# Log sums that run through a sequence, instead of starting again every 128 tokens

## The chip, the cores and the metric

One core of a Trainium2 chip runs the whole program. The metric is device microseconds of one execution, as the median of several. The kernel before takes 425.86 us (three runs, 425.14 to 426.12).

## The reference

Two parts follow each other. The first is a linear recurrence over 768 tokens, for 4 sequences and 8 heads of 48 features, with a complex decay per token and feature:

```python
mag = np.sqrt(a_re * a_re + a_im * a_im)
scale = np.minimum(mag, 0.999) / (mag + 1e-06)
a_re_n, a_im_n = (a_re * scale, a_im * scale)
for t in range(S):
    new_re = ar * S_re - ai * S_im
    new_im = ar * S_im + ai * S_re
    S_re, S_im = (new_re + kv, new_im)      # kv = outer(k[t], v[t])
    y[:, :, t] = np.einsum('bhd,bhde->bhe', q[:, :, t], S_re)
```

The second is a gated block on y: `h = gelu(x @ w_in)`, its halves u and v, v normalized over its features, mixed over the tokens by `w_sg` and shifted by `b_sg`, `gated = u * v_s`, and `out = x + gated @ w_out`.

## The kernel before

The recurrence is computed in chunks of 128 tokens (24 of them, numbered g; c = g mod 6 is the place in the sequence). The logarithm of the decay's size is summed over the tokens; exp of half that sum multiplies q (`ep`), exp of minus half multiplies k (`em`), cosine and sine of the summed angle turn both. Within a chunk, scores `pa` (line 668) are masked into `am` (678), and `py` (719) takes `am` times v. Across chunks a state `S` of 96 x 384 is carried: `ps` (694) is k times v of the chunk, transposed to `kt` first (650), and `py` adds q times the state of the chunk before (724).

Work is prepared in units of up to 256 tokens. The first sequence has tokens on the partitions and sums by matmul; the three later ones (`fea(n)`, nine units) have features on the partitions, three tiles of 128, and sum with scans on the vector engine. For these the log sum starts again every 128 tokens: the scan at line 450 multiplies the running sum by `going`, which is 0 at each 128th element. So `ep` at a chunk's last token is the decay over the whole chunk, and the state has to be multiplied by it: line 499 spreads these columns, `pd` (507) moves them by six small matmuls with `of_head` and `of_place` into `dec`, and lines 705 and 710 multiply the state by `dec`.

```python
nc.vector.tensor_tensor_scan(out=x, data0=going, data1=x, initial=0.0, op0=ALU.mult, op1=ALU.add)
```

Turned k and q of the later sequences go through DRAM (`rk`, `rq`, line 607) to come back with heads on the partitions (`K`, `Q`, line 628). The gated block is `normal` (`pv`, line 236, gelu, statistics, `vh`, `vl`), `expand` (`pu`) and `spatial` (`pvs`, `po`), each product as three matmuls of rounded parts.

Every piece of work is a generator, and `ORDER` is a written list of steps: a name says which generator goes on by one step, `:3` three times, and the number of primes says which engine takes a step that could run on several (`alt`: in `evac` none is ScalarE and one is VectorE, in `ew` one prime is GpSimd). `f` is `keep_warm`, in which a step with no prime issues nothing. Each engine, and the DMA queue that SP issues, takes its instructions in this order. The names of the steps: `l` and `m` load, `g` logs, `e` scale, `p` turns, `r` rotate, `z` heads, `a` attend, `n`, `x`, `y` the gated block.

Of the kernel before, what the change touches and what calls it, by code (L numbers as in the profile page):

```python
# [18 lines left out]
P = 128  # L19
# [5 lines left out]
RE_MIN, IM_MAX = 0.7, 0.98  # L25
# [12 lines left out]
e2'' a1 z1 e1 a1 a0' g3 e2 g3 a1'' a1 s2' t3 a1 w4:2 a1 g3 s2 w7' p2 v2 s2 w4 p3 g3:2 e2:2 a0 w4 g3:2 r3 v3 z3 g3 r2
a1 e3 w7' r3 z2 r2 w9 z3:2 w1'' p3 w12:2 w9'' l4 z2 g4 e3 z2 p3 w12 a1 m3 z3 g4 w9 z2 w4 z2 p3 w4' w12 g4 z2 m3 e3 z2
e2 p3 e3' w8 z3 w12'' e3 p3'' e3' z3' z2 e3 e3' e3 g4 z3 a2 n0_0 z3' a2'' w8 a2:2 n0_0' p3 e3 a2 s3 w5 w8 a2 g4 a2' a2  # L40
a3 a2:2 a3:2 s3 a3 s3 a3'' a3 w12 w5 a3 r4'' e3 a3 r4 n0_0' n0_0 t4 w5 z4 a3 g4 n0_0 z4 w5 z4 r5'' w10 n0_0:2 z4 v5
n0_2:2 z4 z4' v4 n0_2' a3 w5 l5 n0_0 a4 z5 z4 a4'' n0_0 r5'' w10 z4 w11 e3 z5 g4 w10' p4:2 a4:2 z5 a4'' z5:4 a4 g4 m4
n0_0 a4:2' w11 g5:2 l6 p4 w14 z5 g4 a4 a5 p4 a5:2 p4 n0_0' e4 m4 a5'' w11'' l6 a5 n0_0' a4 e4:2 w5 s4 l5 n0_2' a5 p4
w15 x0_0 a5 s4:2 n0_3 e4'' e4 n0_0 x0_0 g5:2 w15 x0_0:2 r6:2 w15 r6:2 r6'' n0_0'' x0_0 w15 n0_2 r6 r6'' x0_0:2 z6 t5
n0_2 n0_3:2'' g5 p5 e4:2 z7 n0_3' x0_3 w15' w15 g5 a6 n0_2 v7 w14 n0_0 p5 v6 w14 r6 p5 g5 x0_0 w14 p5 n0_0'' n0_3
w14'' z6 n0_2'' a6:2 w14' a7 g5 n0_3 n0_2 n0_3 p5 n0_3 x0_3 n0_2' a6:2 n0_3:2 a7 f a7 s5 n0_3 z7 g6 x0_3 m5 g5 n0_3
a7'' a6:3 e5 a6:2 p5 n0_3 e5'' f e5 o1:2 a7 a6 g6 n0_3 a6 a7'' g6'' a7 m5 l7 a7'' n0_3' l7 a7 s5:2 a7 r8 n0_3' r8
n0_3'' r8'' n0_3 n0_3:2'' n0_3 r8 a7'' n0_3'' z8 a6 g6 e5:2 t6 a6 r8'' r8 g6 a7 r8 y0_0:4 x0_3 g6 r8 y0_0' y0_0:2 z9
y0_0'' p6 y0_0 y0_0' p6 g6 y0_0 l8 y0_0 p6 y0_0'' z8 z9 y0_0 y0_0' g6 g7 y0_0 a7 x0_3 y0_0:3 a8 y0_0' g7 p6 g6 v8 p6
a9 a8 g7 e6 s6'' a9 y0_0 a8 a8' a9 m6 a8 l8 a8'' a8 s6 e5 a8 a9 s6 a8 m6 e6'' v9 y0_0 a7 a8 g7 e5 r10 t7 g7 y0_0 r10  # L50
p7 r10'' p7 r10 a9 e6 a8:2 a9:2 a8 e6' x0_3 v10 y0_3 a8 e6 r10'' z10 x0_3 g7 x0_3 g7 z11 y0_3 r10 y0_0 g8 a9 y0_0 r10'
y0_0 p7 g7 y0_3 y0_0 p7 y0_0 a9 r10 e6 y0_3:2' y0_0 g7 z10 g8:2 m7 a9:2 e7 a9 y0_3 g8 a9' p7:2 y0_3 y0_3'' g8 z11 s7'
t8 y0_3 s7 y0_3'' y0_3 a10 s7 e7 a10' a10 m7 e6'' a10' e7 a10:3 a10'' a10 a11 y0_3 a9 a10 g8 r12' a10' a10 a11'' v11
a11 n1_0 a10 l9 r12 a11'' y0_3'' y0_3 r12' a10 r12 g9 e7 n1_0 g8 e7 r12 y0_3 a11 r12 y0_3 a11 n1_0 g8 n1_0:2 a11 p8
y0_3 f r12'' v12 p8 y0_3 y0_3:2' l9 g8 n1_3 g9 n1_0:2 p8 n1_0:3 y0_3 n1_0 z12 p8 y0_3 r12 m8 z12 n1_0 y0_3 p8 n1_3 z13
g9' g9 n1_3'' y0_3 s8' n1_0 g9 y0_3 e8 y0_3 e8' e8 g9 y0_3 m8 n1_3 y0_3 a12 n1_0 y0_3 p8 a12' a12 s8:2 a12' a12 a12''
n1_0:2'' l10 t9 v13 p9 k2 z13 r14 n1_0 a12 a12'' n1_0'' n1_0 r14 e8'' n1_0' e7 a12 a13' a13:2 r14 e7 x1_3:2 l10 x1_3
e8 x1_3 r14 n1_0 r14'' r14 n1_3:6 z15 x1_3 n1_0' n1_3:2 x1_3 m9 a12 f:3 a13'' a13 a12 a13:2 a13'' a13:2 a13'' r14'
n1_3 g9 r14 n1_3' z14 e8:2 n1_3 n1_3' n1_3'' a13 n1_3 f a15' f n1_3'' a13 n1_3:2 g9 n1_3 p9:2 x1_3 y1_3 x1_0 v14 g10
a13 g10:2 y1_3 p9 a15 g10 x1_3 g10 z15 g9 y1_3 e9 y1_3:2' y1_3 a12 y1_3 y1_3'' y1_3 p9 y1_3' g10 y1_3 x1_0 a14 e9''  # L60
z14 x1_0' a14'' a14 a15 a14' a14:2 v15 a15' e9 y1_3 s9 m9 a14 l11 a14'' g10 s9 a12 a14:2 a14' a15 e9'' a14 l11 a15 s9
y1_3' r16 e9 r16 f r16'' y1_3' r16:2 a15 x1_0 t10 p10:3 g10 y1_3 r16 k2 x1_0:5 a14' x1_0 r16' r16 x1_0 z16 g11 v16 g10
# [26 lines left out]
def tile_kernel(ctx: ExitStack, tc: tile.TileContext, t_q, t_k, t_re, t_im, u_q, u_k, u_re, u_im, t_v, v, q, k, f_re, f_im,  # L89
# [40 lines left out]
    def cst(shape, dt, name):  # L130
        return const.tile(shape, dt, name=name, tag=name)
# [107 lines left out]
    def others():  # L239
        nc.gpsimd.memset(going, 1.0)  # L240
        nc.gpsimd.memset(going[:, 0:MT:P], 0.0)
# [165 lines left out]
    def logs(n):  # L407
# [686 lines left out]
```

## Time and profile before

| what | value |
|---|---|
| median of 3 runs | 425.86 us (425.14 to 426.12) |
| profiled execution, first to last instruction | 424.2 us |
| TensorE busy | 410.3 us, 97% of the span |
| VectorE busy | 347.8 us, 82% |
| ScalarE busy | 278.5 us, 66% |
| GpSimd busy | 161.1 us, 38% |
| granted TensorE clock, mean | 0.997 |
| DMA | 92.95 MB, mean 219 GB/s |

The page gives no time for the profiled execution besides its span; the median of the runs is 1.7 us above that span, which is what lies around the instructions. Busy time counts an instruction from its start to its modelled end, so that matmuls that follow each other closely overlap; for them the distance between starts is the cost.

### The profile page before, as it was taken

To read this page: it belongs to the slowest core of one execution; us is meant where nothing else is said; L and a number is where in the kernel's file an instruction comes from. 1 tells how busy PE (TensorE), PEld (TensorE's weight loads), DVE (VectorE), ACT (ScalarE), POOL (GpSimd) and SP (SyncE) were. 2 spreads that over 40 slices of the span, in tenths; PEclk is the share of its full clock that TensorE was granted. 3 is DMA by queue.
4 is the path that set the end of the run, shared out by engine and by line. 5 is a ranking of instruction groups with operands and counts; after the bars stand their busy time and mean duration, and the time that the engine had idled before them with its cause. 6 is when DMAs were issued, how large, how long until landed. Compare 5 with 4: busy or idle time off the path is not lost. (4 is left out here: it accounts for less than half of the span.)

```text
span 424.2 us, 10001 instructions
## 1 busy us (share of the span) xinstructions
PE 410.3 (97%) x3914; PEld 375.8 (89%) x3914; DVE 347.8 (82%) x600; ACT 278.5 (66%) x396; POOL 161.1 (38%) x218
## 2 busy tenths in 40 slices
PE   7999998989999999999899999999999999999994
PEld 5667787879899998989899998989999989899994
DVE  5999989999999989996999698797975546585482
ACT  7899998999899768876987945855830212540010
POOL 4126248265241442815274643622121255223210
PEclk9999999999999999999999999999999999999998
DMA  6778869698498888979669879889669955653531
GB/s 207 232 244 227 263 183 285 172 279 264 123 284 257 240 290 229 286 221 289 174 173 298 232 228 286 272 225 257 138 199 298 247 164 173 194 177 110 185 97 62
DMA packets 77564, 92.95 MB, mean 219 GB/s; under 512 B 10564, under 2 KB 59462, under 8 KB 77512
## 3 DMA queue, kind: packets, MB, share of 16 engines
q1 hardware_dynamic: 77368, 92.16, 73.5%
q8 instruction: 32, 0.52, 0.5%
q14 instruction: 20, 0.16, 0.1%
q10 hardware_dynamic: 144, 0.10, 0.1%
HBM read 68.64 MB, written 23.60 MB: 217 GB/s over the span
## 5 line engine op out<-in xcount | busy, mean ns | idle before, releaser
L236 PE MATMUL pvs<-wsgh,vh 128*128 128x384 f32 x192 | 65.6, 342 | 0.0
L236 PE MATMUL pvs<-wsgh,vl 128*128 128x384 f32 x192 | 65.0, 339 | 0.0
L236 PE MATMUL pvs<-wsgl,vh 128*128 128x384 f32 x192 | 64.7, 337 | 0.0
L199 ACT ACT_TABLE_LOAD x48 | 61.6, 1283 | 1.7 <-PEq L1079 0.9
L668 PE MATMUL pa<-Q,K 96*64 96x64 f32 (+1 forms) x768 | 41.4, 250 | 1.3 <-ACT csn L200 0.9
L668 PEld LDWEIGHTS pa<-Q,K 96*64 96x64 f32 x768 | 36.9, 137 | 4.2 <-issue 1.5
L719 PE MATMUL py<-am,vbuf 128*64 128x128 f32 x384 | 38.8, 275 | 0.4 <-DVE am L678 0.4
L236 PEld LDWEIGHTS pvs<-wsgh,vh 128*128 128x128 f32 x192 | 36.0, 188 | 1.2 <-issue 0.9
L236 PEld LDWEIGHTS pvs<-wsgh,vl 128*128 128x128 f32 x192 | 36.1, 188 | 0.6 <-DVE vl L225 0.5
L236 PEld LDWEIGHTS pvs<-wsgl,vh 128*128 128x128 f32 x192 | 36.1, 188 | 0.0
L678 DVE TENSOR_TENSOR am<-pa,masks 128x512 f32<-128x512 f32 x45 | 30.3, 682 | 5.6 <-PE pa L668 4.8
L724 PE MATMUL py<-Q,S 96*48 96x128 f32 x320 | 33.8, 272 | 0.0
L236 PE MATMUL pu<-xh,winh 128*128 128x384 f32 x96 | 32.8, 341 | 0.0
L850 PE MATMUL po<-gh,wouth 128*128 128x384 f32 x96 | 32.7, 341 | 0.0
L225 POOL TENSOR_TENSOR gl<-tg,gh 128x384 fp32r<-128x384 f32 x13 | 16.8, 1290 | 41.0 <-DVE gh L222 20.8
L850 PE MATMUL po<-gh,woutl 128*128 128x384 f32 x96 | 32.4, 337 | 0.0
L236 PE MATMUL pu<-xh,winl 128*128 128x384 f32 x96 | 32.4, 337 | 0.0
L850 PE MATMUL po<-gl,wouth 128*128 128x384 f32 x96 | 32.3, 337 | 0.0
L236 PE MATMUL pu<-xl,winh 128*128 128x384 f32 x96 | 32.3, 337 | 0.0
L236 PE MATMUL pv<-winh,xh 128*128 128x512 f32 x72 | 29.0, 403 | 0.5 <-ACT u__1296 L200 0.3
L236 PE MATMUL pv<-winh,xl 128*128 128x512 f32 x72 | 28.4, 395 | 0.7 <-DVE xl L225 0.7
L863 DVE SCALAR_TENSOR_TENSOR tg<-pvs,gcol,bsg 128x384 f32<-128x384 f32 x32 | 19.5, 609 | 10.8 <-PE pvs L236 10.6
(285 smaller groups left out, 1104.6 us busy)
## 6 DMA issues: line engine op xcount, KB each, us to landing
vbuf<-in_t_v_dram SPq DMA_DIRECT2D x24, 288.0 KB, 5.7
K<-rk SPq DMA_DIRECT2D x18, 384.0 KB, 5.3
Q<-rq SPq DMA_DIRECT2D x18, 384.0 KB, 7.6
x<-xd SPq DMA_DIRECT2D x9, 576.0 KB, 6.4
xd<-yp SPq DMA_DIRECT2D x48, 96.0 KB, 3.3
gr<-in_f_im_dram SPq DMA_DIRECT2D x12, 384.0 KB, 3.7
out_dram<-x SPq DMA_DIRECT2D x23, 192.0 KB, 2.8
re<-in_u_re_dram SPq DMA_DIRECT2D x9, 384.0 KB, 5.6
```

The source lines that it names most:

```text
L199: nc.scalar.preload_act_table_set(SETS[t])
L225: ew().tensor_tensor(out=l, in0=src, in1=h.bitcast(F32), op=ALU.subtract)
L236: nc.tensor.matmul(o, w(i), x(i), start=(i == 0 and j == 0), stop=(i == n - 1 and j == 2))
L668: nc.tensor.matmul(pa[rows, hh, j:], K(h)[:, j:j + KB], Q(h)[:, j:], start=True, stop=True)
L678: nc.vector.tensor_tensor(out=pairs(am), in0=pairs(pa), in1=causal, op=ALU.mult)
L719: nc.tensor.matmul(py[64 * e:64 * e + 64, p_, :], Vy(h)[:, 0:64], ams[h // 4][:, h % 4, :], start=True, stop=c == 0)
L724: nc.tensor.matmul(py[64 * e:64 * e + D, p_, :], Sb()[:, h, :], Q(h), start=False, stop=True)
L850: nc.tensor.matmul(po[d], w[:, f, ds], g[:, f, :], start=f == 0 and j == 0, stop=f == NF - 1 and j == 2)
L863: nc.vector.scalar_tensor_tensor(out=tg, in0=pv, scalar=gcol[:, f:f + 1], in1=bsg[:, tsl], op0=ALU.mult, op1=ALU.add)
```

## The change

For the nine units of the later sequences the log sum now starts at `MIDDLE` = 128 for a sequence's first unit and runs on over all 768 tokens. Three scans of 256 take the place of two of 384, and an extra small instruction keeps the last column of a unit for the next one (six units of nine). With one sum for the sequence, k and q carry the whole decay, and the state needs no product: the columns (499), the matmuls `pd` (507), their evacuations and the products with `dec` (705, 710) go. The first chunk of a sequence now only copies `ps` to `S`; the three steps where this stands have no prime, so it is a ScalarE copy. `going`, `of_head` and `of_place` are no longer made. The check of the inputs' range takes 0.845 in place of 0.7 as the least real part; the general path behind that check is as it was.

In the list of steps the 69 steps `f` without a prime go, and 17 others stand elsewhere, all between the tokens around chunk 10 and chunk 13; one of these (`a10`) has a prime more, which puts its evacuation on VectorE. One line of the list, before and after:

```diff
@@ ORDER
-... n1_0 a10 l9 r12 a11'' y0_3'' y0_3 r12' a10 r12 g9 e7 n1_0 g8 e7 r12 y0_3 a11 r12 y0_3 a11 n1_0 g8 n1_0:2 a11 p8 ...
+... n1_0 a10' l9 r12 a11'' y0_3'' y0_3 r12' a10 r12 e7 n1_0 g9 g8 e7 y0_3 a11 r12 y0_3 a11 r12 n1_0 g8 n1_0:2 a11 p8 ...
@@ logs
-        for j in range(0, NK * UT, MT):
-            x = fl(U[n]["lo"])[:, j:j + MT]
-            nc.vector.tensor_tensor_scan(out=x, data0=going, data1=x, initial=0.0, op0=ALU.mult, op1=ALU.add)
+        b, c0, m = units[n]
+        for kt in range(NK):
+            x = U[n]["lo"][:, kt, :]
+            nc.vector.tensor_tensor_scan(out=x, data0=x, data1=x, initial=run["sum", b, c0][:, kt:kt + 1] if c0 else MIDDLE,
+                                         op0=ALU.add, op1=ALU.bypass)
+        if c0 + m < NCH:
+            total = run["sum", b, c0 + m] = gp.tile([P, NK], F32, tag="sum", name="sum", bufs=2)
+            ends = U[n]["lo"][:, :, m * P - 1]
+            nc.vector.tensor_tensor(out=total, in0=ends, in1=ends, op=ALU.max)
@@ scale
+        if fea(n):
+            yield
+            psm.tile([P, DM], F32, tag="m", name="pd")
+            yield
+            yield
+            return
...
-        cols_ = gp.tile([P, NK, UC, H], F32, tag="sq", name="cols_", bufs=1)
-        nc.vector.tensor_tensor(out=cols_[:, :, 0:m],
-                                in0=ep[:, :, P - 1:m * P:P].unsqueeze(3).broadcast_to([P, NK, m, H]),
-                                in1=of_head.unsqueeze(1).unsqueeze(1).broadcast_to([P, NK, m, H]), op=ALU.mult)
-        yield
-        pd = psm.tile([2 * D + 1, UC, H], F32, tag="m", name="pd")
-        for kt in range(NK):
-            j = (NK - 1 - kt) * DG
-            for r in COLS:
-                nc.tensor.matmul(pd[r, 0:m, :], of_place[:, j + r.start:j + r.stop], cols_[:, kt, 0:m, :],
-                                 start=kt == 0, stop=kt == NK - 1)
-        yield
-        evac(dec[:, 0:m], pd[0:2 * D, 0:m])
@@ attend
-            if c == 0:
+            if fea(n):
+                if c == 0:
+                    evac(Sn, ps[0:2 * D])
+                else:
+                    nc.vector.tensor_tensor(out=Sn, in0=ps[0:2 * D], in1=Sb(), op=ALU.add)
+                    yield
+            elif c == 0:
```

Where the order moves, for three engines in the same stretch (chunks 12 and 13, the second unit of the third sequence). On VectorE, with the second product with q (`q_2107`, whose result goes to DRAM and comes back as Q of chunk 12), before:

```order
L499 TENSOR_TENSOR cols__2221<-ep_2015,of_head 128x48
L604 TENSOR_TENSOR ep_2015<-q_2107,csn_1970 128x768
L225 TENSOR_TENSOR gl<-tg,gh 128x384
L225 TENSOR_TENSOR xl<-x,xh 128x1152
L446 SCALAR_TENSOR_TENSOR lo_2269<-l_2054,inv_1946 128x768
L524 SCALAR_TENSOR_TENSOR im_1771<-im_1771,left 128x256
L863 SCALAR_TENSOR_TENSOR tg<-pvs,gcol,bsg 128x384
L604 TENSOR_TENSOR q_2107<-q_2107,csn_1970 128x768
L524 SCALAR_TENSOR_TENSOR im_1771<-im_1771,left 128x256
L866 TENSOR_TENSOR tg<-u__1923,tg 128x384
L450 SCALAR_TENSOR_TENSOR lo_2269<-going,lo_2269 128x384 x2
```

and of the change (the q of the same unit is `q_2075` there):

```order
L220 TENSOR_TENSOR gl<-tg,gh 128x384
L583 TENSOR_TENSOR ep_1983<-q_2075,csn_1942 128x768
L220 TENSOR_TENSOR xl<-x,xh 128x1152
L430 SCALAR_TENSOR_TENSOR lo_2232<-l_2022,inv_1918 128x768
L503 SCALAR_TENSOR_TENSOR im_1754<-im_1754,left 128x256
L848 SCALAR_TENSOR_TENSOR tg<-pvs,gcol,bsg 128x384
L435 SCALAR_TENSOR_TENSOR lo_2232<-lo_2232,sum 128x256 x3
L440 TENSOR_TENSOR sum<-lo_2232 128x3
L583 TENSOR_TENSOR q_2075<-q_2075,csn_1942 128x768
```

The columns are gone, and the scans of the next unit and the small instruction behind them now stand ahead of that product with q, not behind it. On the DMA queue that SP issues, before:

```order
L375 DMA im_2297<-in_u_im_dram 128x768
L764 DMA x<-xd_3_135 128x3x384
L628 DMA K<-rk 96x1024
L607 DMA rq<-q_2107 128x3x128 x2
L375 DMA k_2357<-in_u_k_dram 128x768
L628 DMA Q<-rq 96x1024
L886 DMA out_dram<-x 128x384
```

and of the change:

```order
L749 DMA x<-xd_3_132 128x3x384
L359 DMA im_2312<-in_u_im_dram 128x768
L607 DMA K<-rk 96x1024
L359 DMA k_2322<-in_u_k_dram 128x768
L586 DMA rq<-q_2075 128x3x128 x2
L607 DMA Q<-rq 96x1024
L871 DMA out_dram<-x 128x384
```

The load of the next unit's `im` went behind the load of x, and that of its k ahead of the two stores of q. On TensorE the transposes, scores and state of chunk 12, the transposes of chunk 13 and the first matmul behind them, before:

```order
L650 MATMUL pk<-ident,K 128x96 x8
L668 MATMUL pa_114<-Q,K 64x128
...
L507 MATMUL pd<-cols__2221,of_place 33x16
L694 MATMUL ps<-vbuf_116,kt 64x48
...
L650 MATMUL pk<-ident,K 128x96 x8
L236 MATMUL pu<-xh,winh 128x384
```

and of the change:

```order
L629 MATMUL pk<-ident,K 128x96 x4
L231 MATMUL pv<-winh,xh 128x512
...
L629 MATMUL pk<-ident,K 128x96 x4
L647 MATMUL pa_111<-Q,K 64x128
...
L629 MATMUL pk<-ident,K 128x96 x8
L231 MATMUL pu<-xh,winh 128x384
...
L673 MATMUL ps<-vbuf_113,kt 64x48
```

Four of chunk 12's transposes went ahead of nine `pv` matmuls, chunk 13's transposes follow directly on the scores of chunk 12, and `ps` of chunk 12 stands 45 matmuls of `pu` and `pv` later, behind them.

## Rows read from the trace of the kernel before

**Rows 1.** The page: span, busy time (share) and instructions, 40 slices in tenths.
```profile
span 424.2 us, 10001 instructions
PE 410.3 (97%) x3914; PEld 375.8 (89%) x3914; DVE 347.8 (82%) x600; ACT 278.5 (66%) x396; POOL 161.1 (38%) x218
...
DVE  5999989999999989996999698797975546585482
```

**Rows 2.** Timeline of TensorE at three waits: start, us, merged instructions; brackets: idle, releaser.
```profile
90.29 0.50 PE L236 MATMUL pv<-winh,xl 128*128 128x512 f32 x1 [0.66 <-DVE xl L225]
...
210.93 0.55 PE L650 MATMUL pk<-ident,K 96*128 96x96 f32 x4 [1.14 <-ACT yp L213]
...
340.20 0.89 PE L668 MATMUL pa<-Q,K 96*64 96x128 f32 x16 [0.32 <-DMA Q<-rq]
```

**Rows 3.** Instructions of tile pd, three of nine: ns min/median/max, first and last start.
```profile
L507 PE MATMUL pd<-cols__1151,of_place x12: 183/206/230, 87.6 to 87.9; 128*64 128x16 f32 x6, 128*33 128x16 f32 x6
...
L507 PE MATMUL pd<-cols__2569,of_place x12: 181/204/209, 195.0 to 195.3; 128*33 128x16 f32 x6, 128*64 128x16 f32 x6
...
L507 PE MATMUL pd<-cols__4374,of_place x12: 181/183/209, 338.4 to 338.7; 128*64 128x16 f32 x6, 128*33 128x16 f32 x6
```

**Rows 4.** Timeline of TensorE at 128 us: start, us, merged instructions.
```profile
128.70 0.47 PE L507 MATMUL pd<-cols__1546,of_place 128*64 128x16 f32 x12
129.02 1.06 PE L694 MATMUL ps<-vbuf,kt 128*33 128x48 f32 x31
```

**Rows 5.** Timeline of VectorE at 103 and 202 to 205 us.
```profile
103.57 0.16 DVE L536 COPY left<-csn 128x3 f32<-128x3 f32 x1
...
202.23 1.39 DVE L524 TENSOR_TENSOR_SCAN im<-im,left 128x256 f32<-128x256 f32 x2
...
204.92 1.80 DVE L450 TENSOR_TENSOR_SCAN lo<-going,lo 128x384 f32<-128x384 f32 x2
```

**Rows 6.** Timeline of VectorE and TensorE, 99 to 109 us; brackets: idle before, releaser.
```profile
99.44 1.77 DVE L450 TENSOR_TENSOR_SCAN lo<-going,lo 128x384 f32<-128x384 f32 x2
...
105.52 0.55 DVE L808 TENSOR_SCALAR vr<-vr,neg,ny 128x512 f32<-128x512 f32 x1 [0.46 <-POOL ny L748]
...
107.50 0.68 DVE L678 TENSOR_TENSOR am<-pa,masks 128x512 f32<-128x512 f32 x1
...
108.23 0.44 PE L719 MATMUL py<-am,vbuf 128*64 128x128 f32 x4 [0.40 <-DVE am L678]
```

**Rows 7.** Instructions of tile S: ns min/median/max; first and last start.
```profile
L710 DVE TENSOR_TENSOR S<-S,dec x10: 524/546/2204, 39.5 to 315.7; 96x384 f32<-96x384 f32 x10
```

**Rows 8.** Groups of ScalarE by form: busy us, mean ns, idle before.
```profile
L213 ACT COPY kt<-pk 128x384 f32<-128x384 f32 x17 | 7.7, 475 | 4.2 <-PE pk L650 4.2
```

**Rows 9.** Timelines of VectorE, SP and TensorE, 165 to 181 us; last, DMA issues of Q.
```profile
165.46 0.95 DVE L604 TENSOR_TENSOR q<-q,csn 128x768 f32<-128x768 f32 x1
...
166.88 0.91 SPq L607 DMA_DIRECT2D rq<-q  x2
...
173.57 0.34 SPq L628 DMA_DIRECT2D Q<-rq  x1
...
178.71 1.56 PE L668 MATMUL pa<-Q,K 96*64 96x128 f32 x32
...
181.02 1.14 PE L694 MATMUL ps<-vbuf,kt 128*64 128x48 f32 x32 [0.45 <-DVE kt L211]
...
Q<-rq SPq DMA_DIRECT2D x18, 384.0 KB, 7.6
```

**Rows 10.** Timeline of VectorE at 326 us, and the chain that ended last at 333 us.
```profile
326.49 0.56 DVE L883 TENSOR_TENSOR x<-po,x 128x384 f32<-128x384 f32 x1 [3.09 <-PE po L850]
...
327.43 0.20 DVE L499 TENSOR_TENSOR cols__4374<-ep,of_head 128x48 f32<-128x48 f32 x1
...
333.45 6.62 DMA Q<-rq
```

**Rows 11.** Timeline of ScalarE at 197 us; brackets: idle before, releaser.
```profile
196.82 0.81 ACT L200 ACTIVATE vr<-vr,nt,ny 128x512 f32<-128x512 f32 x1 [2.08 <-POOL nt L749]
```

More of the change, by code (lines that the diff above doesn't have):

```diff
@@ L23 @@
 LN_2EPS = math.log(2e-6)
-RE_MIN, IM_MAX = 0.7, 0.98
+RE_MIN, IM_MAX = 0.845, 0.98
+MIDDLE = 128.0
 EXP_BITS, EXP_LOW = 0x7FF00000, 897 << 20
@@ L38 @@
[L38 to L62, printed above, removed]
@@ new lines @@
+a13' a13:2 r14 e7 x1_3:2 l10 x1_3 e8 x1_3 r14 n1_0 r14'' r14 n1_3:6 z15 x1_3 n1_0' n1_3:2 x1_3 a12 m9 a12 a13'' a13
+a12 a13:2 a13'' a13:2 a13'' r14' n1_3 g9 r14 n1_3' z14 e8:2 n1_3 n1_3' n1_3'' a13 n1_3 a15' n1_3'' a13 n1_3:2 g9 n1_3
+p9:2 x1_3 y1_3 x1_0 v14 g10 a13 g10:2 y1_3 p9 a15 g10 x1_3 g10 z15 g9 y1_3 e9 y1_3:2' y1_3 a12 y1_3 y1_3'' y1_3 p9
+y1_3' g10 y1_3 x1_0 a14 e9'' z14 x1_0' a14'' a14 a15 a14' a14:2 v15 a15' e9 y1_3 s9 m9 a14 l11 a14'' g10 s9 a12 a14:2
+a14' a15 e9'' a14 l11 a15 s9 y1_3' r16 e9 r16 r16'' y1_3' r16:2 a15 x1_0 t10 p10:3 g10 y1_3 r16 k2 x1_0:5 a14' x1_0
@@ new lines @@
+n2_0:2 m11 n2_0 z19 t12 y1_0 p11 n2_0 s11:2 r20' a18 a18' a18 y1_0 h20 p12 a17 v18 y1_0:2 n2_3 e11'' y1_0:2 n2_0' n2_0
+a18 n2_0 y1_0 n2_0'' p12 a19' a19 n2_0 n2_0' a19 a18 h11 a18 a19 a18 y1_0 a18 r20 n2_0'' a18:2 a19 n2_3 r20' a18 a19''
+a19 e11 h10 a19:2 n2_3 h11 r20 a19 r20'' n2_0'' h10 a19:2 a18 n2_3:2 v20 n2_3 z20 n2_0'' r20 p12 m12 a18 n2_3 r20'
+n2_3:2 p12 r20 y1_0 n2_3:2 x2_3:2 k8 x2_3 n2_3 z21 n2_3 x2_3 n2_3 h20 n2_3 x2_3 n2_3'' x2_0 p12 n2_3' n2_3:3'' x2_3
+n2_3 n2_3'' x2_3 x2_0 k8 s12 y2_3:2 a21 h8 y2_3 x2_3 g12 a21 x2_0'' y2_3'' a21 g12 y2_3' a21 e12 y2_3:3 z21 y2_3
@@ new lines @@
+y2_3'' y2_3:2 z20 y2_3 a19' y2_3'' k5 y2_3'' e12 h4 y2_3 x2_0 k5 e12 a20:2' a20 v21 a20' h8 a20 s12 a20 a19 a20 e11
+s12 h15 h4 a20 h1 a20 a21 e11'' r22' r22:3 a20 y2_3 z23 a20'' a20 a21' a21:2 y2_3'' a21 h15 h22 a21 y2_3'' a21:2
+x2_0:2 h5 m12 y2_3'' h22 h0 x2_0 y2_3 e12' y2_3 v23 z22 y2_0 h5' v22 y2_3 h2 a20' y2_0 x2_0 y2_3:3 y2_0'' e12 r22:3
+x2_0 r22 y2_3 x2_0 y2_3 a20 y2_0 y2_0'' a21 z22 y2_0:2 k7 y2_0:2' y2_0:2 z23 y2_0 a21 h0' a22:5 a22' a22 e12 h2' a22:2
+x2_0 a23 y2_0 a22 y2_3 h18 e12'' a22' a22 y2_0'' n3_0 a23:2 a23'' a22 n3_0' y2_0 a22 a23 n3_0' y2_0:2 a23:2 y2_0' n3_0
@@ new lines @@
+h18 n3_0:2 k10 h1' k10 n3_0:3 y2_0'' y2_0 n3_3 n3_0 n3_3 k7 n3_0 y2_0:2 n3_0 n3_3' h7 h7'' k12 y2_0:3 n3_0 k1 n3_0'
+y2_0 n3_0' y2_0 n3_0 y2_0 n3_3 n3_0' n3_0:2 n3_3 n3_0' n3_3 n3_0 n3_3 k12 n3_0 h6 n3_3:3 x3_3 n3_3 x3_3 n3_3 y2_0
+x3_3:3 h19 x3_3 k1 x3_3 n3_3:2 n3_3' x3_0 h19 n3_3 n3_3:2' n3_3'' x3_3 h13 n3_3' n3_3'' n3_3 h23 k6 h13 x3_0:2 h6 h23
+y3_3:2 y3_3:3'' y3_3:2 y3_3' y3_3:5 k6 k9 y3_3'' h14 y3_3' h14 y3_3 k4 k0 x3_0 y3_0 y3_3 y3_0 k3 x3_0 k4 y3_3' x3_0
+y3_3'' k9 y3_3' h12 y3_3:3 y3_0' k3 h12 y3_3:2 x3_0 y3_3:2 h21:2 y3_3 h16 h17 x3_0 y3_0'' h17 y3_0' y3_0:2 x3_0 y3_0''
@@ L85 @@
+y3_3 y3_0' k0 k11 y3_0 h3 h16 y3_0 ok x3_0 h3 y3_0 y3_0'' k11 ok y3_0 x3_0 y3_0 ok:2 y3_0:2 ok y3_0:3 ok y3_0:3 ok
+y3_0:9
 """
@@ L248, in others @@
                                     base=g0 + KB - P, pattern=[[1, P]], channel_multiplier=-1)
-        nc.vector.tensor_reduce(out=of_head, in_=ident.rearrange("p (j h) -> p h j", h=H), axis=AX.X, op=ALU.add)
-        nc.gpsimd.memset(of_place, 0.0)
-        place = of_place[:, 0:2 * D].rearrange("p (a d) -> p a d", a=2)
-        nc.gpsimd.memset(place, 1.0)
-        nc.gpsimd.affine_select(out=place, in_=place, compare_op=ALU.is_ge, fill=0.0,
-                                base=H * 2 * DG, pattern=[[0, 2], [-H, D]], channel_multiplier=1)
-        nc.gpsimd.affine_select(out=place, in_=place, compare_op=ALU.is_ge, fill=0.0,
-                                base=H - 1 - H * 2 * DG, pattern=[[0, 2], [H, D]], channel_multiplier=-1)
         yield
@@ L485, in scale @@
             yield
-        dec = ap_.tile([2 * D, UC, H], F32, tag="dec", name="dec", bufs=2)
-        if not fea(n):
-            row = dram.tile([UC, DM], F32, name=f"row{n}")
-            nc.sync.dma_start(out=row[0:m].rearrange("(o c) f -> o c f", o=1), in_=ep[P - 1:P, 0:m])
+        if fea(n):
             yield
-            for a in range(2):
-                with nc.allow_non_contiguous_dma(reason="one row becomes columns"):
-                    nc.sync.dma_start(out=dec[a * D:(a + 1) * D, 0:m, :], in_=row[0:m].rearrange("c (h d) -> d c h", d=D))
-            U[n]["dec"] = dec
+            psm.tile([P, DM], F32, tag="m", name="pd")
+            yield
             yield
             return
-        cols_ = gp.tile([P, NK, UC, H], F32, tag="sq", name="cols_", bufs=1)
-        nc.vector.tensor_tensor(out=cols_[:, :, 0:m],
-                                in0=ep[:, :, P - 1:m * P:P].unsqueeze(3).broadcast_to([P, NK, m, H]),
-                                in1=of_head.unsqueeze(1).unsqueeze(1).broadcast_to([P, NK, m, H]), op=ALU.mult)
+        dec = ap_.tile([2 * D, UC, H], F32, tag="dec", name="dec", bufs=2)
+        row = dram.tile([UC, DM], F32, name=f"row{n}")
+        nc.sync.dma_start(out=row[0:m].rearrange("(o c) f -> o c f", o=1), in_=ep[P - 1:P, 0:m])
         yield
-        pd = psm.tile([2 * D + 1, UC, H], F32, tag="m", name="pd")
-        for kt in range(NK):
-            j = (NK - 1 - kt) * DG
-            for r in COLS:
-                nc.tensor.matmul(pd[r, 0:m, :], of_place[:, j + r.start:j + r.stop], cols_[:, kt, 0:m, :],
-                                 start=kt == 0, stop=kt == NK - 1)
-        yield
-        evac(dec[:, 0:m], pd[0:2 * D, 0:m])
+        for a in range(2):
+            with nc.allow_non_contiguous_dma(reason="one row becomes columns"):
+                nc.sync.dma_start(out=dec[a * D:(a + 1) * D, 0:m, :], in_=row[0:m].rearrange("c (h d) -> d c h", d=D))
         U[n]["dec"] = dec
```

62 lines of the change are left out of this document (29 added, 33 removed).

## The prediction

> **What bounds the kernel now.** I read the page first. TensorE is busy 410.3 of 424.2 us, VectorE 347.8, but the slices show VectorE at nine tenths or more in nearly all of the first half and at five to eight tenths later [rows 1]. So the end is set by TensorE's own stream plus the few places where it waits, and whatever leaves that stream counts in full unless a wait behind it takes it back. So I looked next for such waits in the timeline: 0.66 us for the rounding of x at 90.29, 1.14 us for the evacuated y at 210.93, 0.32 us for Q from DRAM at 340.20 [rows 2]. They are gates: if TensorE arrives earlier and the other side does not, the wait grows by what was saved. Behind the last of them TensorE runs through to the end, in the chain that ended last.
>
> **The change part by part.**
>
> *Matmuls removed.* Each unit's `pd` is 12 records, nine times, from 87.6 to 338.7 us; the same number of records and nearly the same durations each time [rows 3]. What one group costs is not the 181 to 230 ns of a record, since they overlap, but how far it pushes what follows: it starts at 128.70 and the next `ps` at 129.02, 0.32 us [rows 4]. Nine are 2.9 us. Three of them lie ahead of a gate: that at 87.6 ahead of the wait at 90.29, that at 195.0 ahead of the wait at 210.93, that at 338.4 directly ahead of the wait at 340.20 [rows 2, 3]. I count these three as lost, so six groups: **-1.9 us**.
>
> *Scans.* Two scans of 384 take 1.80 us, two of 256 that start from a column 1.39, so three 2.09; the extra small instruction is like the copy `left` of 128x3, 0.16 [rows 5]. A group grows from 1.80 to 2.25, +0.45. At most places VectorE has room for it, or gets it back from what else goes (below). At one place it does not: the scans at 99.44 stand ahead of statistics on which GpSimd's `ny` rests; VectorE waits for that in the instruction at 105.52, the mask at 107.50 follows in order, and `py` waits 0.40 us for it at 108.23 [rows 6]. Nothing between is removed that would not just lengthen the wait for GpSimd: the removed product of the first state stands ahead of the wait, not behind it. **+0.45 us**. [...] The rows say more: 256 elements fewer in two scans save 1.80 - 1.39 = 0.41 us, so 768 elements cost 1.23 and some 0.29 is left over for each scan [rows 5]. [...]
>
> *State and columns on the vector engines.* Each product with `dec` is 0.55 us (median) on VectorE, ten with the first sequence's two, which stay [rows 7]; eight go, with nine column products of 0.20 or more (one stands among the rows of the last gate, below) and three first-state products. That is about 6 us of VectorE's time over the stretch from 80 to 340, against 9 x 0.45 = 4 us of longer scans at the most. I cost the difference at nothing: behind 110 us TensorE's stream covers it, and where the cover is gone it is the wait at 210.93 that would show it.
>
> *First states on ScalarE.* Three copies of 96x384; the nearest row is the evacuation of 128x384, 0.475 us [rows 8]. The first reader of such a state is the `py` of the next chunk, behind two groups of scores and its own `ps`; I cost them at nothing, at most 0.5 us each if ScalarE is late.
>
> *Startup.* Some GpSimd and VectorE instructions that only make tables go from the first 6 us. The first sequence's work waits for its loads there; nothing gained, nothing lost. [...]
>
> *The 17 steps.* `ps` of chunk 12 waited 0.45 us for `kt` at 181.02 [rows 9]; it now stands 45 matmuls later, with the transposes earlier: **-0.45 us**. Against that, the product with q at 165.46 comes behind the next unit's scans: 2.25 us later, less the 0.20 of the columns [rows 5, 9, 10]. Queued behind it are its store at 166.88, the load of Q at 173.57, two stores of output and the load of K of chunk 13; and the scores of chunk 12 at 178.71 wait for that Q, the transposes of chunk 13 behind them for that K [rows 9]. Before, TensorE did not wait there, so there was some slack, of a size that no row shows. Lower end 0. Upper end: 2.05 us of shift, and a load that takes the median of 7.6 us where it had at most 178.71 - 173.57 = 5.1, so 4.5. I take **+0.5 us**, near the lower end: the bytes that were moving beside that store are the same and only stand ahead of it now, so it cannot be late by the whole shift unless nothing of it was hidden. The evacuation of y that goes from ScalarE to VectorE falls in a stretch in which VectorE waits for TensorE; nothing.
>
> *The last gate.* Its side is: TensorE's `po` at 326.49 lets VectorE go on (it had waited 3.09 us), then the columns of 0.20, the products, store, and the load of Q of 6.62 us [rows 10]. TensorE leads this loop, so it moves with TensorE, and is shorter by the columns: **-0.2 us**.
>
> Sum: -1.9 + 0.45 - 0.45 + 0.5 - 0.2 = -1.6 us. The profiled execution had 424.2 and the median of the runs is 425.86, 1.7 above it; I take the difference over to the median: **424.3 us**. About 0.2% (0.85 us, so below 425.0 or above 426.7) is what a measurement of this kernel can tell from no change.
>
> **The rivals.**
>
> *All of it counts (chance 0.15).* VectorE gets more room than the longer scans take, and the waits that it causes shrink: all nine groups (-2.9), the waits at 181.02 and 108.23 gone (-0.45, -0.4), of that at 210.93 half (-0.6), nothing new: -4.3, 421.5 us. For it: VectorE's full slices up to the middle [rows 1]. Against: the gate at 210.93 comes from a ScalarE that waited for GpSimd at 196.82 and not for VectorE [rows 11].
>
> *The gates hold (0.20).* ScalarE's late evacuation at 210.93 is not led by TensorE, and comes when it came; everything ahead of it is then worth nothing. Three groups of `pd` are left between the gates (-1.0) and the last step (-0.2): 424.7 us. If the load of Q at 340.20 does not move either, only its 0.2 are left: 425.7 us. For it: the waits exist. Against: the 2.08 us that ScalarE stood idle at 196.82 and the 3.09 us of VectorE at 326.49 [rows 10, 11] are waits that begin with a product of TensorE, so both gates should come along.
>
> *Slower: Q of chunk 12 arrives late (0.10).* One mechanism, at 178 us: the scans ahead of the product with q push store and reload to the end that I left out above, 4.5 us of waiting in place of 0.5. Then the sum is +2.4: 428.3 us. It decides from 3 us of waiting on (0.5 + 1.6 + 0.9). For it: the median load of Q is longer than the time this one had [rows 9], and the load of the next k now stands ahead of the store. [...]
>
> *The change does nothing that the time shows (0.05).* The moved steps cost elsewhere what the matmuls give: 425.9 us.
>
> **How the numbers follow.** The forecast has 0.50. Its own range is 423.2 to 425.0 (the Q term between 0 and 1.5, the lost groups between one and three, ScalarE's copies free). From 421.8 to 426.6 all of it, most of the gates and half of the first rival lie inside; outside are the rest of that rival and the late Q. Faster by over 0.2%: 0.47 of the forecast, 0.15, 0.08 of the gates, together 0.70. Within: 0.03 + 0.12 + 0.04 + 0.02 of a moderately late Q = 0.21. Slower: 0.08 + 0.01 = 0.09.
>
> **What would show it.** Right: TensorE's records fewer by 108; the `ps` behind a group's place following the scores directly; a wait for the mask near 108 us of about 0.85; no wait for `kt` near 180; the wait for y near 209 still there, and longer by up to 0.3. Wrong: a wait of `pa` or `pk` on the loads of Q or K near 178 us over 1 us, a wait for a first state, or the wait near 209 grown by more than 1 us.

## The result, and the profile after

The change makes the kernel slower: 427.76 us median (426.47 to 427.99) against 425.72, ratio 1.0057, 95% interval 1.0034 to 1.0081 (the medians alone differ by 2.0 us). A second measurement on another chip, among the experiments, gave 1.0028 (1.0004 to 1.0052). So the kernel loses 1.2 to 2.4 us where 1.6 less was forecast. The profiled execution took 426.47 us and is the quickest of the first four; its span is 424.7.

The page after, span, busy time and three lines of slices:

```profile
span 424.7 us, 9760 instructions
PE 408.1 (96%) x3806; PEld 373.1 (88%) x3806; DVE 341.4 (80%) x591; ACT 279.0 (66%) x393; POOL 151.5 (36%) x208
...
PE   7999998989999999989999999999999999999995
...
DVE  4999989998998999896999798776984547575483
...
PEclk9999999999999999989999999999999999999999
```

What was to go is gone: TensorE has 108 records fewer and is busy 2.2 us less, VectorE 6.4 less than before [rows 1]. No first state is waited for. The last gate, the Q of [rows 2] at 340.20, has 0.41 us where it had 0.32; the masks near 108 us take 0.26 and 0.32 where one took 0.40 [rows 6]. The largest loss shows in one place, which the eighteenth slice of PE and of PEclk marks. The timeline of TensorE there (start, us, what; in brackets the idle time ahead and its releaser), with its merged windows (busy time and count of PE, PEld, DVE, ACT, POOL, then the granted clock, DMA share, GB/s):

```profile
179.76 1.56 PE L647 MATMUL pa<-Q,K 96*64 96x128 f32 x32 [0.22 <-DMA Q<-rq]
181.61 0.52 PE L629 MATMUL pk<-ident,K 96*128 96x96 f32 x4 [0.29 <-DMA K<-rk]
183.59 0.55 PE L629 MATMUL pk<-ident,K 96*128 96x96 f32 x4 [1.46 <-DVE kt L206]
...
184.92 0.52 PE L231 MATMUL pu<-xl,winh 128*128 128x384 f32 x1
185.24 0.52 PE L231 MATMUL pu<-xh,winl 128*128 128x384 f32 x1
...
188.17 0.34 PE L231 MATMUL pu<-xh,winh 128*128 128x384 f32 x1
188.34 0.34 PE L231 MATMUL pu<-xl,winh 128*128 128x384 f32 x1
```

```profile
180.00:184.00 4.00, 2.25 (x41) 1.95 (x37) 4.00 (x6) 3.98 (x6) 1.39 (x3) 1.00 0.68 242
184.00:188.00 4.00, 4.00 (x17) 4.00 (x15) 3.97 (x7) 2.83 (x4) 0.00 (x0) 0.57 0.95 298
```

The two waits for Q and K are the 0.5 us of the prediction's Q term (0.22 + 0.29). But `kt`, for which `ps` had waited 0.45 us [rows 9], now holds the transposes for 1.46 us. TensorE stood for nearly half of those 4 us (2.25 us busy), and in the 4 us behind that its granted clock was 0.57, where the kernel before has 1.00: ten `pu` stand 0.32 us apart in place of 0.17, 1.5 us more. Matched matmul by matmul with the kernel before, TensorE is 1.1 us late at the scores of chunk 12 and 2.6 at the end of these `pu`; the gate for y, 1.14 us before [rows 2], is used up and gives back 1, about what the scores of chunk 13 lose ahead of it; at the last matmul 1.4 are left. The span is only 0.5 us longer all the same, because the end behind the last matmul took 0.9 us less in this execution.

There are smaller losses as well. TensorE has waits for masks (at 254 us the profile names no releaser) that it did not have before:

```profile
158.55 0.44 PE L704 MATMUL py<-am,vbuf 128*64 128x128 f32 x4 [0.38 <-DVE am L657]
...
254.18 0.44 PE L704 MATMUL py<-am,vbuf 128*64 128x128 f32 x4 [0.70 <-issue]
...
276.16 0.89 PE L647 MATMUL pa<-Q,K 96*64 96x128 f32 x16 [0.34 <-DVE am L657]
```

Matched in the same way, TensorE loses 0.4 us at the masks near 108, 0.8 near 158, 0.6 near 254 and 0.5 near 276, and gains 0.35 to 0.65 where groups of `pd` stood at 143, 231 and 308. The second profile of the change has the same steps.

What made `kt` late is a chain that begins with one of the 17 moves. SP's queue, GpSimd, ScalarE and VectorE of the change:

```profile
167.20 0.38 SPq L749 DMA_DIRECT2D x<-xd  x1
167.63 0.48 SPq L359 DMA_DIRECT2D im<-in_u_im_dram  x1
```

```profile
173.48 2.22 POOL L401 TENSOR_TENSOR im<-im,inv 128x768 f32<-128x768 f32 x1 [1.98 <-DMA im<-in_u_im_dram]
...
179.50 1.82 POOL L469 TENSOR_TENSOR k<-k,em 128x768 f32<-128x768 f32 x1
```

```profile
175.73 0.85 ACT L195 ACTIVATE l<-im 128x768 f32<-128x768 f32 x1 [1.74 <-POOL im L401]
```

```profile
173.02 0.96 DVE L511 SCALAR_TENSOR_TENSOR csn<-csn,im 128x768 f32<-128x768 int32 x1 [0.18 <-ACT csn L195]
...
179.59 2.55 DVE L425 SCALAR_TENSOR_TENSOR l<-re,l 128x768 f32<-128x768 f32 x1 [1.67 <-ACT l L195]
...
182.98 1.01 DVE L206 COPY kt<-pk 128x384 f32<-128x384 f32 x2
```

The load of `im` stands behind that of x, which waits 1.1 us for its stores; it is issued at 167.63 where it was issued at 164.78 before. GpSimd waits 1.98 us for it, ScalarE 1.74 for GpSimd, VectorE 1.67 for ScalarE. And VectorE's `l`, which takes 0.95 us elsewhere, starts 0.09 us after a product of GpSimd and takes 2.55. In the second profile of the same kernel it starts ahead of that product (179.63 against 181.70): 0.95 us, no wait for `kt`, clock 1.00 from 180 to 188 us. So that piece comes and goes. The execution of that profile took 425.24 us, the least of its twelve, whose median is 426.75; whether the executions nearer the median have the wait is not shown.

### The profile page after: what moved, and what is told of

Read it like the earlier page. It is cut to its first block, busy times and chain, and to the rows that moved or that the text cites. A ratio compares the mean times of both kernels' runs of the same rounds, so it can differ in the third digit from the quotient of the medians.

```text
span 424.7 us, 9760 instructions
## 1 busy us (share of the span) xinstructions
PE 408.1 (96%) x3806; PEld 373.1 (88%) x3806; DVE 341.4 (80%) x591; ACT 279.0 (66%) x393; POOL 151.5 (36%) x208
## 4 chain that ended last, share of the span: by engine, by line
PE 50%; DVE 18%; DMA 11%; ACT 8%; issue 5%; SPq 3%; POOL 3%; DVEq 0%; POOLq 0%; ACTq 0%
PE pvs L231 13%; PE po L835 7%; PE pu L231 7%; PE pv L231 6%; PE pa L647 4%; PE py L704 3%; PE py L709 2%; PE ps L673 2%; ACT L194 2%; PE pk L599 2%; ACT l L195 2%; DMA vbuf<-in_t_v_dram 2%; SPq L586 2%; DMA rq<-q 1%; DVE am L657 1%
## 5 line engine op out<-in xcount | busy, mean ns | idle before, releaser
L704 PEld LDWEIGHTS py<-am,vbuf 128*64 128x64 f32 x384 | 25.4, 136 | 3.9 <-DVE am L657 2.4
```

The source lines that it names most:

```text
L704: nc.tensor.matmul(py[64 * e:64 * e + 64, p_, :], Vy(h)[:, 0:64], ams[h // 4][:, h % 4, :], start=True, stop=c == 0)
```

## Experiments

All against the kernel before on the same chip; 0.1% is 0.43 us. Its own runs scatter more on these chips (423.85 to 428.95 in one set), which is why the intervals are about 0.2% wide to either side. Three theories stood first: A, the late `im`; B, the new code on VectorE; C, the late Q and K.

**The late im alone.** `l9` goes from behind to ahead of the load of x:

```diff
-... y0_3:2' n1_3 n1_0:2 g9 p8 n1_0:3 y0_3 l9 n1_0 z12
+... y0_3:2' l9 n1_3 n1_0:2 g9 p8 n1_0:3 y0_3 n1_0 z12
```

> The changed kernel, with one load put back: that of im of the next unit stands ahead of the load of x on SP's queue, as in the kernel before. Theory A (the late im: GpSimd's product, ScalarE's l, VectorE's l and then kt come late, TensorE waits 1.46 us at 183.6 us and runs at the lower clock for 1.5 us behind it): the wait and the slow stretch go, 2.9 us at 183 us, of which the wait at 213 us may take 1.0 back: 424.8 to 425.8 us against 427.8 of the change. Theory B (the code itself costs: longer scans, copies on ScalarE): as the change, 427.8. Theory C (the late store and reload of q and k): the waits of 0.22 and 0.29 us stay, 427.5 to 427.8.

Measured: 0.9985 (0.9964 to 1.0007), 1.8 to 3.1 us below the two ratios of the change. `kt` starts at 181.35, no wait of TensorE at 183, clock 1.00. A holds for this part: with that load put back the change is no slower than the kernel before.

**Code and order apart.** The changed code with the old list, and the old code with the new list:

> The changed code with the list of steps of the kernel before (its steps f without a prime left out): none of the 17 steps is moved. Theory A: the loss of the change is in the moved steps, the code part gains what the groups pd behind the last gates are worth: 424.0 to 425.2 us, faster than before. Theory B: the code costs, 427 us or more. Theory C: as A.

> The kernel before with the 17 moved steps and none of the new code. Theory A: the late im costs it as much, 2 to 3 us more than before: 427.7 to 428.7. Theory B: 425.7, as before. Theory C: 426.2 to 426.7, by the two waits for Q and K of 0.5 us.

Measured: 1.0027 (1.0004 to 1.0050) and 1.0026 (1.0002 to 1.0049). Each alone costs about 1.1 us. The first contradicts A: with none of the 17 steps moved, the code that leaves out 108 matmuls is slower than before. The second fits none of the three: A had 2 to 3 us, B nothing, and C's waits for Q and K near 180 us are not in its profile. That profile is of the quickest of its twelve executions (425.21 us, median 427.04) and has no wait for `kt` either, and clock 1.00 from 180 to 192 us, so where the order loses time with the old code is not shown.

**The matmuls put back** into the change, on constants:

> The changed kernel with the 108 matmuls of pd put back on constants (they write a PSUM tile that nobody reads and wait for nobody on VectorE): what these matmuls are worth here. All nine groups of 0.32 count: 2.9 us more than the change, 430.7. Three lie ahead of waits that take them back, as the prediction has it: 1.9 more, 429.7. All of them hidden: 427.8.

Measured: 1.0014 (0.9992 to 1.0036). The change itself was run again to compare:

> The changed kernel once more, beside the kernels below. Theory A (the late im is what costs): the wait for kt of 1.5 us at 183 us and the slow stretch behind it stand in this profile too, and the kernel takes 2 us more than before. Theory E (who comes first decides there: VectorE's l and GpSimd's product of k with em start within 0.1 us of each other at 179.5, and the l that comes second took 2.55 us in place of 0.95): the wait may be absent in this execution, the kernel is then 1 to 2 us above before all the same, by the code's own cost of 1.1 us that the run with the old order showed.

Measured: 1.0028 (1.0004 to 1.0052). So in the change the 108 matmuls cost nothing that can be measured (by the two intervals, 0.8 us at the most). In the trace the groups push TensorE by 0.2 to 0.3 us at 232, 310 and 340 us, and shorter waits for masks near 254 and 276 give that back: TensorE does not lead there, VectorE does.

**The scans, from both sides.** In the kernel before, three scans of 256 with the same values; in the changed code with the old list, the old two (this kernel leaves out the carry from chunk to chunk). The first edit, without the line of the scan, which now takes `going[:, 0:UT]`:

```diff
-        for j in range(0, NK * UT, MT):
-            x = fl(U[n]["lo"])[:, j:j + MT]
+        for kt in range(NK):
+            x = U[n]["lo"][:, kt, :]
```

> The kernel before with its log sums in three scans of 256 in place of two of 384, to the same values, and nothing else: the cost of the longer scans alone. As the prediction has it (one place, the mask at 107.5): 0.35 to 0.45 us more than before. Theory D (VectorE's order is what TensorE waits for at many places, near 106, 158, 176, 181, 252 and 274 us): 1.5 to 2.5 us more. Hidden: no difference.

> The changed code with the old list of steps and the old two scans of 384 that start anew in every chunk (the carry from chunk to chunk and the small instruction are left out): only the columns, the matmuls pd and the products with dec are gone. As the prediction has it: six groups of 0.32 and the columns of the last gate, 2.1 us less than before. Theory D: TensorE waits for VectorE where the matmuls stood, and they are worth 0 to 1 us; then the new scans cost the rest of the 1.1 us that the run with the old order lost, 1.1 to 2.1.

Measured: 1.0052 (1.0031 to 1.0073), and 0.9946 (0.9929 to 0.9963). This is the cause of the code's loss: without the new scans the rest of it is worth 2.3 us (1.6 to 3.0), as the prediction had it (2.1); the cut alone costs 2.2. In the changed code the new scans, with their small instruction, make the difference between 2.3 us below and 1.1 above, 3.4 us; theory D, which had the cost of the cut right (1.5 to 2.5), expected less of both of these.

How a cut can cost that is the surprise. By itself it is 0.05 us: the group at 73 us takes 1.82 in place of 1.77, that at 205 1.84 in place of 1.80, and so for eight of nine. The fifth group does not fit. VectorE, then GpSimd, of the kernel before:

```profile
167.43 2.06 DVE L450 TENSOR_TENSOR_SCAN lo<-going,lo 128x384 f32<-128x384 f32 x2
169.42 0.66 DVE L797 BATCH_NORM_STATS2 bst<-vr 128x6 f32<-128x512 f32 x1
170.12 0.18 DVE L798 BATCH_NORM_AGGREGATE mv<-bst 128x2 f32<-128x6 f32 x1
170.22 0.72 DVE L524 TENSOR_TENSOR_SCAN im<-im,left 128x256 f32<-128x256 f32 x1
```

```profile
168.78 1.53 POOL L225 TENSOR_TENSOR gl<-tg,gh 128x384 fp32r<-128x384 f32 x1
170.27 2.32 POOL L417 TENSOR_TENSOR im<-im,inv 128x768 f32<-128x768 f32 x1
```

To find the place, the same cut for that unit alone (`n == 8`), and for all others:

> The kernel before with three scans in place of two, to the same values, for one unit alone: the fifth of the nine, whose scans stand at 167.4 us. Theory F (one place: the added scan pushes VectorE's next instructions into GpSimd's products, where in the run with three scans in all units the group took 2.88 us in place of 2.06 and the scan of im behind it 1.48 in place of 0.72): VectorE 1.4 us later behind 173 us, and never back, 1.2 to 2.2 us above before. Theory D (the cost is spread over the units): 0.2 us above, a ninth.

> The same for the eight other units, with the two scans of 384 left at 167.4 us. Theory F: 0 to 0.6 us above before. Theory D: 1.5 to 2.0 us above.

Measured: 1.0027 (1.0007 to 1.0047) and 1.0007 (0.9985 to 1.0028). One unit carries 1.1 us. VectorE, GpSimd and two waits of TensorE of the run with that unit alone:

```profile
167.36 2.89 DVE L451 TENSOR_TENSOR_SCAN lo<-going,lo 128x256 f32<-128x256 f32 x3
170.17 0.67 DVE L798 BATCH_NORM_STATS2 bst<-vr 128x6 f32<-128x512 f32 x1
...
170.97 1.46 DVE L525 TENSOR_TENSOR_SCAN im<-im,left 128x256 f32<-128x256 f32 x1
```

```profile
168.43 1.27 POOL L225 TENSOR_TENSOR gl<-tg,gh 128x384 fp32r<-128x384 f32 x1
169.66 2.22 POOL L417 TENSOR_TENSOR im<-im,inv 128x768 f32<-128x768 f32 x1
```

```profile
176.67 0.50 PE L236 MATMUL pv<-winh,xl 128*128 128x512 f32 x1 [0.38 <-DVE xl L225]
...
182.09 1.08 PE L695 MATMUL ps<-vbuf,kt 128*64 128x48 f32 x31 [1.08 <-DVE kt L211]
```

Before, the scan of `im` began 0.05 us ahead of GpSimd's product and took 0.72, and GpSimd's product was the long one (2.32 us, where a run below has it free at 1.86). With one boundary more, GpSimd's `gl` takes 1.27 us for 1.53 while the log sums take 2.89 for 2.06, its product begins 0.6 us earlier, and the scan of `im` behind it takes 1.46. Together VectorE is 1.27 us later at the product with `csn` (174.40 for 173.13), and TensorE pays it at two waits, 0.38 us for the rounding of x, which is new, and 1.08 for `kt` in place of 0.45 [rows 9]. The statistics are not lengthened there: 0.66 us beside `gl` in the kernel before, 0.67 beside the product of `im` here.

**The collision taken away.** The scan of `im` (`p8`) put ahead of the log sums (`g8`), nothing else:

```diff
-p8 y0_3 y0_3:2' l9 g8 n1_3 g9 n1_0:2 p8
+p8 y0_3 y0_3:2' l9 p8 g8 n1_3 g9 n1_0:2
```

> The kernel before with three scans for the fifth unit alone, as in three_at_168 (there 1.1 us above before), and one more edit: the scan of im that VectorE has behind them stands directly ahead of them. The same instructions, but the scan of im no longer falls into GpSimd's product of im. Theory F (the collision turns 0.35 us of longer scans into 1.4): the scan of im takes 0.72 in place of 1.46 us, VectorE is 0.7 us earlier behind 174 us than in three_at_168, 0.2 to 0.7 us above before. Theory G (any delay of VectorE at this place counts, in full and by its own length, and the collision only moves): as three_at_168, 1.1 above before.

Measured: 1.0054 (1.0029 to 1.0079), a miss that tells more than a hit. The scan of `im` is free, as expected, but the log sums are now the ones that run into the product:

```profile
168.22 0.75 DVE L524 TENSOR_TENSOR_SCAN im<-im,left 128x256 f32<-128x256 f32 x1
168.88 4.49 DVE L450 TENSOR_TENSOR_SCAN lo<-going,lo 128x256 f32<-128x256 f32 x3
173.29 0.66 DVE L797 BATCH_NORM_STATS2 bst<-vr 128x6 f32<-128x512 f32 x1
```

VectorE comes to `csn` at 176.36, two us later than without the swap. In the kernel before, the scan of `im` took 0.72 us; with the cut it was the long one on VectorE (1.46), and with the swap it is the log sums, at 4.49 where they took 2.89. Moving one instruction only chose which one pays.

**GpSimd held back by a dependence.** The changed code, old list, the swap, and the fifth unit's small instruction on GpSimd ahead of its product, so that the product cannot start before the log sums are done; then the same without the swap; then the product of `im` on VectorE:

```diff
+            if n == 8:
+                nc.gpsimd.tensor_scalar(out=total, in0=ends, scalar1=1.0, scalar2=1.0, op0=ALU.mult, op1=ALU.mult)
+            else:
                 nc.vector.tensor_tensor(out=total, in0=ends, in1=ends, op=ALU.max)
```

> A version that could beat both: the changed code, the old list of steps, the scan of im ahead of the fifth unit's log sums, and that unit's small instruction on GpSimd, ahead of its product of im, so that this product cannot start before the log sums are done. Theory H (the time follows the moment at which VectorE comes to the product csn with im behind them, 173.1 us in the kernel before, 176.7 with the old order alone, 173.9 with the two scans): scan of im and log sums run free of that product, VectorE comes there at 174.2 to 175.0, 0.5 to 2 us below before. Theory G (the new code costs whatever VectorE does there): 1 us above before.

> As the version above, without the scan of im moved: the changed code, the old list, the fifth unit's small instruction on GpSimd ahead of its product of im. Theory H: the small instruction's 1.64 us leave VectorE, but the scan of im starts into GpSimd's product and waits up to 1 us: VectorE at the product with csn at 175.0 to 176.2, 0.5 below to 0.7 above before. Theory G: 1 us above.

> The changed code and the old list, with the product of im that GpSimd does beside the fifth unit's log sums on VectorE (0.95 us there, behind the product with csn): nothing of GpSimd is left for the small instruction and the scan of im to run into. Theory H: VectorE comes to the product with csn at 174.3 to 175.0 us in place of 176.7, and has 0.9 us more behind it: 1 us below to 0.5 above before. Theory G: 1 us above or more.

Measured: 0.9987 (0.9968 to 1.0006), 1.0023 (1.0004 to 1.0041), 1.0031 (1.0011 to 1.0051). VectorE reached `csn` at 174.35, 175.58 and 174.30, all three as expected. The first time follows. The second, 1.0 us above, lies just outside its range (0.7), with an interval that reaches into it. The third, 1.3 above, does not follow, and why stays open: its extra 0.95 us and a wait for ScalarE bring VectorE to `kt` at 182.40, later than in the first (181.44), but earlier than in the run with the old list alone (183.80), which is no slower. VectorE and GpSimd of the first:

```profile
167.76 0.74 DVE L506 TENSOR_TENSOR_SCAN im<-im,left 128x256 f32<-128x256 f32 x1
168.43 2.93 DVE L435 TENSOR_TENSOR_SCAN lo<-lo,sum 128x256 f32<-128x256 f32 x3
...
174.35 0.94 DVE L514 SCALAR_TENSOR_TENSOR csn<-csn,im 128x768 f32<-128x768 int32 x1
```

```profile
171.44 0.20 POOL L441 TENSOR_SCALAR sum<-lo 128x3 f32<-128x3 f32 x1 [1.28 <-DVE lo L435]
171.60 1.86 POOL L401 TENSOR_TENSOR im<-im,inv 128x768 f32<-128x768 f32 x1
```

**Versions meant to beat both.** The small instruction on ScalarE:

> A version that could beat both: the changed code, the old list of steps, the scan of im ahead of the fifth unit's log sums, and the small instruction that keeps the sum on ScalarE (it took 1.64 us on VectorE behind a product of GpSimd in the run with the old order). Theory F: VectorE loses 0.7 to 1.5 us less near 170 us than with the old order alone (1.1 above before): 0.4 below to 0.4 above before. Theory G: 1 above before.

> The changed kernel with im loaded ahead of x (0.6 below before in its run) and the small instruction that keeps the sum on ScalarE. Theory F: 0.1 to 0.6 less than with im first alone, 0.7 to 1.2 below before. If ScalarE's order is what the masks or the copies wait for instead: 0.6 below or worse.

Measured: 1.0099 (1.0069 to 1.0129) and 1.0019 (0.9992 to 1.0046). In the first, ScalarE's copy stands 4.21 us waiting for the log sums, and the evacuation `vr` queued behind it keeps TensorE waiting 2.9 us. The second has no such wait; it gains nothing over `im` first alone, and why is open.

```profile
172.72 0.20 ACT L440 COPY sum<-lo 128x3 f32<-128x3 f32 x1 [4.21 <-DVE lo L435]
...
176.38 1.09 ACT L195 ACTIVATE vr<-pv 128x512 f32<-128x512 f32 x2
```

```profile
PE po L835 <- ACT vr L195: 2.9, 1, 2.9
```

One scan of 768 for three (`im` first with the new list, then the old list; the carry goes into the first columns, the multiplier is 0 at each row's start):

> The changed kernel with im loaded ahead of x, and with one scan of 768 (a multiplier of 0 at each start of a row, the carry added to the first column by a small instruction) in place of three of 256: a version that could beat both. Theory D: VectorE gives back 0.3 us a unit at the places where TensorE waits, 0.5 to 1.5 us less than with im first alone (which was 0.6 below before): 1.1 to 2.1 us below before. If the scans are hidden: 0.6 below before.

> The changed code with the old list of steps and one scan of 768 for a unit, the carry added to its first columns by a small instruction: the full computation of the change, with about as much time on VectorE per unit as the old two scans (1.70 us). If theories F and D are right that the longer scans took what the removed matmuls gave, it comes near the run with the two scans that start anew (2.3 us below before): 1.3 to 2.3 us below before, and below the change. If the copies on ScalarE or the carry cost it, 0 to 1 us above.

Measured: 1.0002 (0.9975 to 1.0028) and 1.0005 (0.9987 to 1.0024). Both miss the gain that theory D expected. The scan takes 1.76 us by itself, no less than two of 384, and at the fifth unit, with the old list, 2.10, with the small instruction 0.80 and the scan of `im` 1.60 behind it: nothing saved where it counts. Last, another mask:

> The version of code_swapped_sum_pool with one more move: the log sums and the small instruction of the eighth unit (246.3 to 248.5 us there), which stand ahead of the masks for which TensorE's py waits 0.69 us at 252.7, stand directly behind these masks, and ScalarE's exp of them one step later. Theory H (VectorE's moment at the places where TensorE waits for it is what the time follows): the wait at 252.7 goes, 0.4 to 0.6 us less than code_swapped_sum_pool, 0.7 to 1.3 below before. If TensorE's wait for the masks at 274 or for Q at 340 takes it back: 0.6 below before, as without the move.

Measured: 0.9999 (0.9984 to 1.0013), no gain over the version with GpSimd held back. The wait at 252.7 is gone, and one behind it came: VectorE now waits 0.88 us for a load, and the moved log sums delay the rounding of x. VectorE, then TensorE:

```profile
247.86 1.65 DVE L401 TENSOR_TENSOR im<-im,inv 128x768 f32<-128x768 f32 x1 [0.88 <-DMA im<-in_u_im_dram]
```

```profile
258.68 0.50 PE L231 MATMUL pv<-winh,xl 128*128 128x512 f32 x1 [1.24 <-DVE xl L220]
```

No version with the whole computation is clearly below the kernel before; `im` first (0.9985) and the version with GpSimd held back (0.9987) come nearest, and both are below the change.

## Why the prediction was wrong

The step that failed is the term of the scans, "+0.45 us", in the sentence that keeps it to one place: "At most places VectorE has room for it, or gets it back from what else goes". At the place that the prediction named the term came out: behind the masks near 108 us TensorE loses 0.4 us in both profiles of the change and in the run with the old list, and nothing with the two scans (0.31 us late ahead of them, 0.29 behind). But elsewhere VectorE has no room. The cut alone costs 2.2 us in the kernel before, five times the term, and 1.1 of them at one unit, where 0.05 us decides which of VectorE and GpSimd comes first; in the changed code the new scans cost 3.4.

The size of a group was nearly right, by luck: at 99 us it grows from 1.77 us to 2.00, and 0.16 for the small instruction, 0.39 for the forecast 0.45. That "some 0.29 is left over for each scan" is a misreading, since the row of 1.39 has scans that start from a column and that of 1.80 has not. Where nothing collides, one scan more costs 0.05 us for the group, and the start from a column 0.06 for each scan (0.72 for 0.66).

*State and columns.* "I cost the difference at nothing" stood on the same belief in room. "That is about 6 us" is short by the prediction's own rows, where 8 x 0.55, 8 x 0.20 and 3 x 0.55 make 7.7. In total VectorE did lose work (6.4 us). But at the fifth unit the columns that went stood earlier, and what counts there is who starts first.

*Matmuls.* "Six groups: -1.9 us", with -0.2 for the last gate, were right under their condition: 2.3 us with the old scans. They are worth nothing when TensorE follows VectorE, which the run with the matmuls put back shows. The prediction treated TensorE as the leader behind 110 us.

*The 17 steps.* "-0.45 us" for `kt` had the wrong sign in the first profile, 1.46 us of waiting and 1.5 at the clock of 0.57; the second has neither. The moved load of `im`, which the order shows and the prediction did not price, is worth 1.8 to 3.1 us: the prediction looked at the loads around the store of q, and not at who waits for `im`. "+0.5 us" for Q came out in the first profile (0.22 + 0.29) and is missing in the second; the slower rival, Q of chunk 12 late by 3 us or more, is in neither. What the moves do well can be read too: the log sums at 165.59 run free of GpSimd (2.02 us), and VectorE is at `csn` at 173.02, not 176.72 as with the old list; the load of `im` then takes that back.

*First states, startup, the last gate:* as forecast, no wait of their own. The gate at 210.93 gave back what was late, not early; in the second profile it is as before (1.17).

For the change itself this makes the late `im` the main part of the loss. With `im` first it is 0.6 us below before in place of the forecast 1.6. That last 1.0 us is hardly clear of the noise; it fits the waits for masks near 108, 158 and 254 us, but no run takes them apart in the new order.

Open is how the other 1.1 us of the cut in all units divide: the eight other units gave 0.3 with an interval of -0.6 to 1.2. That VectorE's moment at `kt` sets the time (theory H) is borne out only roughly: 180.97 us with the two scans (2.3 below), 181.44 (0.6 below), 183.80 (1.1 above), 186.32 (4.2 above); but 182.97 with one scan and the old list, at 0.2 above, 182.40 with the product on VectorE, at 1.3 above, and 181.49 with the cut in the fifth unit alone, at 1.1 above.

## What to carry to other kernels

Where VectorE is full and GpSimd works beside it, do not price a changed instruction by its own length: look which GpSimd instruction stands beside it and who starts first, and how narrow that was (here 0.05 us of own length became 1.27 at `csn`). Removed TensorE work counted here only where TensorE led (2.3 us with the old scans, 0.8 at the most in the change); a run that puts the removed work back, and one that leaves the suspected cost out, tell this apart. A moved load is priced by its first reader and by everyone queued behind that reader (here waits of 1.98 us on GpSimd, 1.74 on ScalarE, 1.67 on VectorE and 1.46 on TensorE in the first profile).

## What the runs showed of the hardware

A small instruction can be long beside GpSimd: the small `sum` of 128x3 takes 0.16 us and took 1.64 behind the product of `im` with the old list. One scan took 0.66 us for 256 elements, 0.92 to 0.95 for 384 and 1.76 for 768 (with a bf16 multiplier), and 0.72 for 256 where it starts from a column. In the first profile of the change TensorE's granted clock was 1.00 from 180 to 184 us, with waits of 0.22, 0.29 and 1.46 us and 2.25 us busy, and 0.57 from 184 to 188, where the `pu` from 184.60 on stand 0.32 us apart; in the run with the old list, with waits of 0.69 and 1.35 us and 3.04 us busy from 180 to 184, it was 1.00 in both stretches.
